# One-core causal attention and squared-ReLU MLP: v's loads as four operations of their own, and a last output block turned on TensorE

## The chip, the cores and the metric

The kernel runs on one core of one Trainium2 chip. The metric is the device time of one execution in microseconds (us); "the time" of a kernel is the median over its runs.

## The reference, cut to what matters

```python
# q, k, v: (4, 12, 448, 64); w_in: (768, 2048); w_out: (2048, 768), all float32
scores = (q @ k.transpose(0, 1, 3, 2)) / 8
scores = np.where(np.triu(ones, k=1), -1e9, scores)
attn = exp(scores - max(scores)); attn = attn / (sum(attn) + 1e-9)
o = attn @ v
x = o.transpose(0, 2, 1, 3).reshape(1792, 768)
h = np.maximum(x @ w_in, 0.0)
out = (h * h) @ w_out                      # (1792, 768)
```

## The kernel before, in words

**The work.** Attention goes by pairs of heads: pair n (0 to 23) is batch n // 6 and heads 2 (n % 6) and the next. For each pair the kernel loads q and k by eight DMAs in 32-column strips (`load_qk`, L343, four for k and four for q, 56 KB each), turns them in 32 x 32 blocks on VectorE (`transposed`, L366), makes scores on TensorE (`scores`, L381 to L388), takes the maximum on VectorE (L399), the exponential on ScalarE (L403), divides on GpSimd or VectorE (L412, L414), turns the probabilities on TensorE (`transposed_p`, L426), copies them out of PSUM (L433, which calls L311, or L434) and multiplies by v (`times_v`, L446). Pairs 0 to 11 (two batches) come first, with two sets of buffers; pairs 12 to 23 run between the matmuls of the MLP.

v is loaded for three pairs at a time (NV = 3) into one of two buffers, by `load_v` (L355), in pairs 0, 3, 6, 9, ...: four DMAs, one for each block of 128 keys (kc), 192 KB for a full one and 96 KB for the last, in rows of 256 bytes, all issued by one operation on SP's queue.

The MLP keeps every float32 operand as two parts (high and low) in float32r, and a product is three matmuls. The first half of the rows goes straight through it in four groups of 512 of the 2048 hidden columns (`h_unit`, L628; `o_unit`, L1000). The weights come in pieces (`piece`, L560): w_in has six pieces c = 0 to 5 a group. A piece's words are loaded (L587; 512 KB for w_in, 384 KB for w_out), ScalarE makes two parts of them (L590, L593, both by way of L311), VectorE puts them together (L595 to L598), and `split` (L327) makes high and low. The second half of the rows goes by a scheme with seven products for eight (`h_pair`, L803; `o_seven`, L949). For the last group `o_last` (L978) makes the eight products as they are: twelve blocks, three (d) for each of four quarters (k) of the sums; a block is twelve matmuls (L941 to L943). Its sum is added on VectorE (L986, which calls L314) to the tile of sums, turned on VectorE in 32 x 32 blocks (L988), and stored by four DMAs in rows of 128 bytes (L993), two on SP's queue and two on ScalarE's. The last block is (k, d) = ("22", 2).

**What sets the order.** Each step is an operation of a planner (`Plan.op`, L72) with a rank (a due time in us), the engines that it may run on with a modelled length, and keys that it reads and writes. `Plan.emit` (L100) walks through time: among the operations that are ready it takes the one that can start first, and among equals the one of lowest rank; a DMA is held back while more than a set backlog (L46) is under way. `take=` reserves a buffer and `drop=` gives it back. The instructions are then put out in that order, and each engine and each queue works through its own in order. Nearly all loads are on SP's queue ("DMA"), a few at the start and some stores at the end on ScalarE's ("DMA2").

Pair n has the time n x 8.6 for n below 12 (PAIR, L1037). Its k and q have that time less 14 as rank (L349). Its v has the time less 4 for n = 0 and less 10 after that (L364). The load of w_in's piece c in group 0 has 10 + 97.2 x (c + 0.5) / 6 - 12 (L1056, L587), but there are only three buffers for the words. `times_v` reads the whole v buffer as one key.

The buffers of the last stages are made late: `grow` (L1102), an operation on POOL of no modelled length, opens a pool in place of an older one.

Of the kernel before, what the change touches and what calls it, by code (L numbers as in the profile page):

```python
# [9 lines left out]
F32 = mybir.dt.float32  # L10
# [5 lines left out]
ALU = mybir.AluOpType  # L16

PE, ACT, DVE, POOL, DMA, DMA2 = range(6)
# [6 lines left out]
class Hold:  # L25
# [5 lines left out]
    @property  # L31
    def t(self):
        t = self.tile[1]
        return t() if isinstance(t, FunctionType) else t
# [127 lines left out]
def t_act(n, psum=False, more=0):  # L162
    return n / 1200 + (0.17 if psum else 0.215) + 0.15 * more


def t_dve(n, fast=False):
    return n / 1920 + 0.15 if fast else n / 960 + 0.15
# [13 lines left out]
def t_dma(count, size):  # L181
    return count * (0.0084 + size * 0.0000488) / 16
# [3 lines left out]
def kernel(  # L186
# [17 lines left out]
    nc = tc.nc  # L204
    B, H, S, D = q.shape
    DM = out.shape[1]
    DFF = w_in.shape[1]
    P = 128
    QC = P // 2
    NQ = S // QC  # L210
    NK = -(-S // P)
    NP = H // 2
    NPH = B // 2
    T = 2 * S
# [3 lines left out]
    CH = DM // 2  # L218
# [14 lines left out]
    TURNED = [(c, kc) for kc in range(NK) for c in range(2 * kc, NQ)]  # L233
    TOFF = [P * next(i for i, t in enumerate(TURNED) if t[1] == kc) for kc in range(NK)]
    NV = 3
    NA = 2 * NP
    PCW = max(GF * P, CH)
    NRAW, NZ, NB, NR = 3, 3, 1, 6
# [2 lines left out]
    CB = NP // 2  # L241
# [18 lines left out]
    plan = Plan()  # L260

    def tiles(nm, n, shape, dtype, pool=const):
        return [pool.tile(shape, dtype, name=f"{nm}{i}") for i in range(n)]

    early = ExitStack()
    pool = early.enter_context(tc.tile_pool(name="early", bufs=1, side="right"))
    ident = pool.tile([P, 3 * QC], F32, name="ident")
    mask = pool.tile([P, S], F32, name="mask")
    even = Buffers("a", pool)
    v_t = tiles("v", 2, [P, NK, 2 * NV, D], F32, pool)  # L270
    x_t = tiles("x", NA, [P, 2, S], F32R)
    wi_t = const.tile([P, 2, NP, GF * P], F32R, name="wi")
# [28 lines left out]
    for i in range(2):  # L301
        m = mask[i * QC:(i + 1) * QC, S - QC:]
        nc.gpsimd.affine_select(
            out=m, in_=m, pattern=[[-1, QC]], base=0,
# [5 lines left out]
    def on_act(n, dst, src, psum=False, func=AF.Copy, more=0, **kw):  # L310
        return (ACT, t_act(n, psum, more), lambda: nc.scalar.activation(dst(), src(), func, **kw))  # L311

    def on_dve(n, dst, a, b, op, more=0.0):
        return (DVE, t_dve(n) + more, lambda: nc.vector.tensor_tensor(out=dst(), in0=a(), in1=b(), op=op))  # L314
# [22 lines left out]
    def attention(s, n, at):  # L337

        b, hp = divmod(n, NP)
        nm = s.nm  # L340
        spare = (lambda us: us) if n >= NA else (lambda us: 0.0)

        def load_qk(key, src, t, j):  # L343


            queue, eng = (DMA2, nc.scalar) if n < 2 and key == "q" else (DMA, nc.sync)
            for h in range(D // SQ):
                i = (j * D + h * SQ)
                plan.op(at - 14, [(queue, 0.5, lambda h=h, i=i: eng.dma_start(  # L349
                    out=t[i:i + SQ].rearrange("p (b d) -> p b d", d=SQ),  # L350
                    in_=src[b, 2 * hp + j, :, h * SQ:(h + 1) * SQ].rearrange(
                        "(b p) d -> p b d", p=SQ),
                ), t_dma(S, 128))], [], [(nm, key, j, h)])

        def load_v():  # L355
            hold = vs[n // NV] = Hold("v", "v")

            def go():
                for kc in range(NK):
                    rows = min(P, S - kc * P)  # L360
                    nc.sync.dma_start(
                        out=hold.t[:rows, kc],
                        in_=v[b, 2 * hp:2 * (hp + NV), kc * P:kc * P + rows].rearrange("h p d -> p h d"))
            plan.op(at - (10 if n > 1 else 4), [(DMA, 0.5 * NK, go, t_dma(2 * NV * S, 256))], [], [hold], take=hold)  # L364

        def transposed(key, src, dst, at):  # L366
            plan.op(at, [(DVE, t_dve(S), lambda: nc.vector.transpose(dst, src))],
# [69 lines left out]
        def times_v(av, at):  # L437

            first = 2 * (n % NV)

            def go():
                for kc in range(NK):
                    m = NQ - 2 * kc
                    p = s.pt[:, TOFF[kc]:TOFF[kc] + m * P].rearrange("p (c j i) -> p c j i", j=2, i=QC)
                    for j in range(2):
                        nc.tensor.matmul(  # L446
                            av.t[j * D:(j + 1) * D, kc * P:S], vr.t[:, kc, first + j], p[:, :, j],
                            start=kc == 0, stop=kc == NK - 1, skip_group_check=True,
                        )
            plan.op(at, [(PE, 0.2 + 4 * sum((S - kc * P) / 2400 for kc in range(NK)), go)],  # L450
                    [vr] + [(nm, "pt", i) for i in range(len(TURNED) // 4)], [av], take=av, drop=[vr],
                    lag=spare(1.0))

        for j in range(2):
# [1 line left out]
        for j in range(2):  # L456
            load_qk("q", q, s.q, j)
        if n % NV == 0:
            load_v()
        vr = vs[n // NV]  # L460
        transposed("k", s.k, s.kt, at)
        transposed("q", s.q, s.qt, at + 1)
        at += 4
        groups = (ORDER[:3], ORDER[3:]) if n < NA else (ORDER,)
        for chunks in groups:
# [11 lines left out]
        av = Hold("ps", "av")  # L477
# [3 lines left out]
        at += 3  # L481
        if n < NA:
            x = x_t[n]
# [5 lines left out]
        else:  # L489
            spill(n - NA, av, at)  # L490

# [51 lines left out]
    late = {"wo": None, "acc": None}  # L543
# [389 lines left out]
    def o_sum(k, d):  # L933
        return lambda: late["sum"][("u2", "11", "12", "21", "22").index(k) * CB + d]

    def o_product(ps, pairs, d, begin, end, rank, step):

        for m, (w, g) in enumerate(pairs):
            def go(w=w, g=g, start=begin and m == 0, stop=end and m == len(pairs) - 1):
                o = ps.t[:, :S]  # L940
                nc.tensor.matmul(o, w.t[:, 0, d], g.t[:, 0], start=start, stop=False, skip_group_check=True)  # L941
                nc.tensor.matmul(o, w.t[:, 0, d], g.t[:, 1], start=False, stop=False, skip_group_check=True)  # L942
                nc.tensor.matmul(o, w.t[:, 1, d], g.t[:, 0], start=False, stop=stop, skip_group_check=True)  # L943
            plan.op(rank, [(PE, 3 * t_mm(S), go)], [(w, 0), (w, 1), (g, 0), (g, 1)], [ps],
                    take=ps if begin and m == 0 else None, drop=[w, g])
            rank += step
        return rank
# [30 lines left out]
    def o_last(W, rank, step):  # L978

        for k in ("11", "21", "12", "22"):  # L980
            i, j = k
            for d in range(CB):
                ps, a = Hold("ps", "os"), o_sum(k, d)
                rank = o_product(ps, [(W[i + m, u], g7[TURNS[-1], m + j, u]) for m in "12" for u in range(2)],
                                 d, True, True, rank, step)
                plan.op(rank, [on_dve(S, a, lambda ps=ps: ps.t[:, :S], a, ALU.add)], [ps], [("sum", k, d)], drop=[ps])  # L986
                h = Hold("f", "tr")
                plan.op(rank, [(DVE, t_dve(S) + 0.05, lambda h=h, a=a: nc.vector.transpose(h.t, a()))],  # L988
                        [("sum", k, d)], [h], take=h)
                row, col = T + (int(j) - 1) * S, (int(i) - 1) * CH + d * P  # L990
                for s in range(P // SQ):
                    def go(eng, h=h, s=s, row=row, col=col):
                        return lambda: eng.dma_start(  # L993
                            out=out[row:row + S, col + s * SQ:col + (s + 1) * SQ].rearrange(
                                "(b p) d -> p b d", p=SQ),
                            in_=h.t[s * SQ:(s + 1) * SQ].rearrange("p (b d) -> p b d", d=SQ))
                    plan.op(rank, [(DMA, 0.6, go(nc.sync), t_dma(S, 128)), (DMA2, 0.6, go(nc.scalar), t_dma(S, 128))], [h], [], drop=[h])
        return rank

    def o_unit(gr, t, ch, rank, step, after):  # L1000
        ps = Hold("ps", "mm")
# [38 lines left out]
    odd = Buffers("b", stack.enter_context(tc.tile_pool(name="b", bufs=1)))  # L1040
    for n in range(NA):
        attention((even, odd)[n % 2], n, n * PAIR)
# [37 lines left out]
    rank, begin = start, 10.0  # L1080
    rest = NG * (2 * GF * NP * H_US + 2 * NT * GF * O_US) - GF * NP * H_US
    for gr in range(NG):
        begin, rank = group(gr, rank, (rest + NA * 7.0) / rest, begin)
# [18 lines left out]
    def grow():  # L1102
        middle.close()
        pool = ctx.enter_context(tc.tile_pool(name="third", bufs=1, reuse_waits="tile"))
        late["g"] = tiles("g3_", 4, [P, 2, S], F32R, pool)
        late["w"] = pool.tile([P, 2, CB, P], F32R, name="w3")
        late["f"] = tiles("f3_", 4, [P, S], F32, pool)
        late["sum"] += tiles("sb", 4 * CB, [P, S], F32, pool)

    grown = over(plan.ops[:mark] + [attended], lent_w[2 * GF:] + lent_f[-1:] + lent_r + lent_g, grow)  # L1110
# [10 lines left out]
    for gr, u in stages:  # L1121
        last = gr == TURNS[-1]
        if u is None:
            W = o_parts(gr, rank - LEAD, rank + 42 * H_US - LEAD)
            rank = o_last(W, rank, H_US) if last else o_seven(gr, W, rank, H_US)
        else:
            W = w_parts(gr, u, rank - LEAD, rank + 7 * CB * H_US - LEAD)
            rank = h_pair(gr, u, W, rank, H_US, last)
# [33 lines left out]
```

## Time and profile before

| | us |
|---|---|
| median of three runs | 615.32 |
| the runs | 617.53, 615.32, 612.15 |
| the profiled execution | 616.32 |
| its span, first to last instruction | 614.5 |
| TensorE matmul busy in it | 589.6 (96%) |
| VectorE, ScalarE, GpSimd busy | 442.8, 357.3, 353.8 |
| mean granted TensorE clock | 0.994 |

The profile is one execution, taken by the hardware profiler. All times in it count from the first instruction. An engine's idle time ahead of an instruction is given in brackets with what ended it. Engines: PE is TensorE, DVE is VectorE, ACT is ScalarE, POOL is GpSimd, SP is SyncE; "SPq" and "ACTq" are instructions of a queue that issue DMAs; L12 is line 12 of the kernel. The granted clock is a share of TensorE's full 2.4 GHz; the lower level, 1.2 GHz, reads 0.5. Matmuls overlap each other, so a matmul's own time is longer than its distance from the next.

### The profile page before, as it was taken

The numbers are of one execution on the slowest core, as the hardware profiler recorded it, in microseconds if no ns is written. First come the engines' busy times: TensorE is split into PE (matmuls) and PEld (weight loads), VectorE is DVE, ScalarE is ACT, GpSimd is POOL, SyncE is SP. The second block draws the span as 40 slices with busy tenths as digits, with TensorE's granted clock in tenths as the row PEclk, the third lists the DMA queues.
The fourth block names the chain that finished last, engine by engine and source line by source line (L and its number), as shares of the span: only waits on it lengthen the run. The fifth ranks groups of instructions, "written<-read, shape, count | busy, mean of one in ns | idle before, by whom it ended". The sixth has DMA issues, their size and how long they took to land.

```text
span 614.5 us, 11394 instructions
## 1 busy us (share of the span) xinstructions
PE 589.6 (96%) x3714; PEld 511.1 (83%) x3714; DVE 442.8 (72%) x958; ACT 357.3 (58%) x878; POOL 353.8 (58%) x459
## 2 busy tenths in 40 slices
PE   3897999999999999999999999999999999999996
PEld 1564677789988988888898889988889999999995
DVE  4888785466786689785787327678996688779754
ACT  3797888656677855578455552255675743652400
POOL 2557575475579746788644764325894666575200
PEclk9899999999999999999999999999999999999999
DMA  8897745597989999989997477867877847863555
GB/s 141 174 208 134 170 105 117 107 306 259 245 230 263 283 267 213 272 254 298 242 282 249 158 204 221 283 196 208 190 139 173 207 120 145 184 151 66 166 91 90
DMA packets 203148, 120.01 MB, mean 195 GB/s; under 512 B 138960, under 2 KB 191056, under 8 KB 203088
## 3 DMA queue, kind: packets, MB, share of 16 engines
q1 hardware_dynamic: 181328, 108.01, 64.2%
q0 software_dynamic: 6912, 9.44, 10.3%
q10 hardware_dynamic: 14848, 1.84, 1.9%
q8 instruction: 29, 0.48, 0.3%
q14 instruction: 31, 0.25, 0.1%
HBM read 80.71 MB, written 38.54 MB: 194 GB/s over the span
## 4 chain that ended last, share of the span: by engine, by line
PE 83%; DVE 7%; DMA 4%; ACT 2%; issue 2%; POOL 1%; SPq 1%; DVEq 0%; ACTq 0%; POOLq 0%
PE ps L1014 7%; PE ps L634 7%; PE ps L1016 6%; PE ps L1015 6%; PE ps L636 6%; PE ps L635 6%; PE ps L426 6%; PE ps L446 6%; PE ps L386 5%; PE ps L941 5%; PE ps L942 5%; PE ps L943 5%; PE ps L819 4%; PE ps L817 4%; PE ps L815 4%
## 5 line engine op out<-in xcount | busy, mean ns | idle before, releaser
L412 POOL TENSOR_SCALAR ap<-ap,asm 128x128 f32<-128x128 f32 (+6 forms) x122 | 72.8, 616 | 53.3 <-DVE asm L471 51.5
L311 ACT ACTIVATE words<-words 128x384 f32<-128x384 f32 (+3 forms) x131 | 75.1, 598 | 28.1 <-DVE words L314 8.3
L399 DVE CUSTOM_DVE_ANT_0 ps<-ps,mask 128x448 f32<-128x448 f32 (+6 forms) x168 | 68.7, 445 | 30.4 <-PE ps L386 23.9
L1014 PE MATMUL ps<-wo,g 128*128 128x384 f32 x224 | 77.0, 344 | 0.0
L634 PE MATMUL ps<-x,wi 128*128 128x448 f32 x192 | 75.0, 391 | 0.6 <-ACT x L311 0.6
L1016 PE MATMUL ps<-wo,g 128*128 128x384 f32 x224 | 75.1, 335 | 0.0
L1015 PE MATMUL ps<-wo,g 128*128 128x384 f32 x224 | 75.0, 335 | 0.0
L636 PE MATMUL ps<-x,wi 128*128 128x448 f32 x192 | 70.8, 369 | 0.4 <-DVE wi L314 0.4
L635 PE MATMUL ps<-x,wi 128*128 128x448 f32 x192 | 70.6, 368 | 0.2 <-DVE x L314 0.2
L318 POOL TENSOR_TENSOR wi<-words,wi 128x384 fp32r<-128x384 f32 (+1 forms) x48 | 62.6, 1326 | 8.8 <-ACT wi L311 6.0
L403 ACT ACTIVATE ap<-ps,mx 128x448 f32<-128x448 f32 (+6 forms) x126 | 58.7, 483 | 13.6 <-DVE mx L399 12.6
L324 POOL TENSOR_SCALAR wi<-words 128x384 fp32r<-128x384 f32 (+1 forms) x44 | 32.0, 730 | 51.6 <-DVE words L598 14.4
L815 PE MATMUL ps<-x,wi 128*128 128x448 f32 x153 | 56.4, 368 | 0.8 <-DVE r L314 0.5
L817 PE MATMUL ps<-x,wi 128*128 128x448 f32 x153 | 56.1, 367 | 0.0
L819 PE MATMUL ps<-x,wi 128*128 128x448 f32 x153 | 56.1, 366 | 0.0
L941 PE MATMUL ps<-g,wi 128*128 128x448 f32 x150 | 55.0, 367 | 0.5 <-ACT sa L311 0.5
L943 PE MATMUL ps<-g,wi 128*128 128x448 f32 x150 | 54.9, 366 | 0.0
L942 PE MATMUL ps<-g,wi 128*128 128x448 f32 x150 | 54.8, 366 | 0.0
L311 ACT ACTIVATE r<-ps 128x448 f32<-128x448 f32 x59 | 32.1, 546 | 38.3 <-PE ps L636 13.6
L314 DVE CUSTOM_DVE_ANT_0 words<-words 128x768 uint16<-128x768 uint16 (+1 forms) x56 | 45.8, 818 | 5.3 <-ACT words L311 1.9
L311 ACT ACTIVATE apt<-ps 128x512 f32<-128x512 f32 x70 | 38.5, 605 | 18.2 <-PE ps L426 18.1
L311 ACT ACTIVATE r<-r 128x448 f32<-128x448 f32 x64 | 36.0, 575 | 14.8 <-DVE r L314 14.0
(140 smaller groups left out, 1475.0 us busy)
## 6 DMA issues: line engine op xcount, KB each, us to landing
words<-in_moe_w_in_dram SPq DMA_DIRECT2D x24, 512.0 KB, 5.5
words<-in_moe_w_out_dram SPq DMA_DIRECT2D x32, 384.0 KB, 4.5
wo_split<-wo SPq DMA_DIRECT2D x26, 384.0 KB, 4.5
wi<-wo_split SPq DMA_DIRECT2D x21, 384.0 KB, 4.0
wo_whole<-words SPq DMA_DIRECT2D x32, 192.0 KB, 3.9
wi_split<-wi SPq DMA_DIRECT2D x24, 256.0 KB, 4.1
v<-in_v_dram SPq DMA_DIRECT2D x24, 192.0 KB, 4.0
wi_whole<-words SPq DMA_DIRECT2D x18, 256.0 KB, 4.6
```

Source lines behind the costliest of these rows:

```text
L311: return (ACT, t_act(n, psum, more), lambda: nc.scalar.activation(dst(), src(), func, **kw))
L634: nc.tensor.matmul(o, w[:, 0], x[:, 0], start=c == 0, stop=False)
L635: nc.tensor.matmul(o, w[:, 0], x[:, 1], start=False, stop=False)
L636: nc.tensor.matmul(o, w[:, 1], x[:, 0], start=False, stop=c == NP - 1)
L815: nc.tensor.matmul(o, w.t[:, 0, c], x[:, 0], start=begin and c == 0, stop=False, skip_group_check=True)
L817: nc.tensor.matmul(o, w.t[:, 0, c], x[:, 1], start=False, stop=False, skip_group_check=True)
L941: nc.tensor.matmul(o, w.t[:, 0, d], g.t[:, 0], start=start, stop=False, skip_group_check=True)
L942: nc.tensor.matmul(o, w.t[:, 0, d], g.t[:, 1], start=False, stop=False, skip_group_check=True)
L943: nc.tensor.matmul(o, w.t[:, 1, d], g.t[:, 0], start=False, stop=stop, skip_group_check=True)
L1014: nc.tensor.matmul(res(), g[:, 0], w[:, 0], start=f == 0, stop=False)
L1015: nc.tensor.matmul(res(), g[:, 0], w[:, 1], start=False, stop=False)
L1016: nc.tensor.matmul(res(), g[:, 1], w[:, 0], start=False, stop=f == GF - 1)
```

## The change

v's loads: `load_v` now makes one operation that only takes the buffer (on POOL, of no length and without an instruction) and four that issue one DMA each. V_AT gives the rank of the first by the pair (0 to -4, as before; from pair 3 on -4 and not -10), and each further one is 2 us later. `times_v` reads the four as four keys.

The last block: `finish` takes the place of the add, the 32 x 32 turn and the four stores. It works in two parts, columns 0 to 255 and 256 to 447 of the block. Each is added on VectorE, turned by two TensorE transposes into a PSUM bank, and copied out: the first part by one copy on ScalarE, the second by two on VectorE. The first part is stored by one DMA on ScalarE's queue (256 rows), the second by two on SP's queue (128 and 64 rows), in rows of 512 bytes. The transposes need an identity, which is made by GpSimd in `grow`.

```diff
+    V_AT, V_STEP = (-4, -10, -4), 2
...
         def load_v():
             hold = vs[n // NV] = Hold("v", "v")
 
-            def go():
-                for kc in range(NK):
-                    rows = min(P, S - kc * P)
+            taken = plan.op(at + V_AT[min(n, 2)], [(POOL, 0.0, lambda: None)], [], [(hold, kc) for kc in range(NK)], take=hold)
+            for kc in range(NK):
+                def go(kc=kc, rows=min(P, S - kc * P)):
                     nc.sync.dma_start(
                         out=hold.t[:rows, kc],
                         in_=v[b, 2 * hp:2 * (hp + NV), kc * P:kc * P + rows].rearrange("h p d -> p h d"))
-            plan.op(at - (10 if n > 1 else 4), [(DMA, 0.5 * NK, go, t_dma(2 * NV * S, 256))], [], [hold], take=hold)
+                plan.op(at + V_AT[min(n, 2)] + V_STEP * kc, [(DMA, 0.5, go, t_dma(2 * NV * min(P, S - kc * P), 256))],
+                        [], [(hold, kc)], [taken])
...
-                    [vr] + [(nm, "pt", i) for i in range(len(TURNED) // 4)], [av], take=av, drop=[vr],
+                    [(vr, kc) for kc in range(NK)] + [(nm, "pt", i) for i in range(len(TURNED) // 4)], [av], take=av, drop=[vr],
...
+                if (k, d) == ("22", CB - 1):
+                    finish(ps, a, d, rank)
+                    continue
...
+    def finish(ps, a, d, rank):
+        row, col = T + S, CH + d * P
+        for first, end in ((0, 2 * P), (2 * P, S)):
+            turned, h = Hold("ps", "os"), Hold("f", "tr")
+            def part(t, first=first, end=end):
+                return lambda: t()[:, first:end]
+            plan.op(rank, [on_dve(end - first, part(a), part(lambda: ps.t), part(a), ALU.add)],
+                    [ps, ("sum", "22", d)], [("sum", "22", d, first)], drop=[ps])
+            def turn(first=first, end=end, turned=turned):
+                for m in range(first, end, P):
+                    n = min(P, end - m)
+                    nc.tensor.transpose(turned.t[:n, m - first:m - first + P], a()[:, m:m + n], late["ident"])
+            plan.op(rank, [(PE, 0.22, turn)], [("sum", "22", d, first)], [turned], take=turned)
+            blocks = [(0, 2, P)] if first == 0 else [(0, 1, P), (1, 1, S - 3 * P)]
+            for m, count, n in blocks:
+                def dst(m=m, count=count, n=n, h=h):
+                    return h.t[:n, m * P:(m + count) * P]
+                def src(m=m, count=count, n=n, turned=turned):
+                    return turned.t[:n, m * P:(m + count) * P]
+                copy = [(DVE, t_dve(P), lambda dst=dst, src=src: nc.vector.tensor_copy(dst(), src()))]
+                plan.op(rank, copy if first else [on_act(2 * P, dst, src, True)],
+                        [turned], [(h, m)], plan.ops[-2:-1] if m else (), take=None if m else h, drop=[turned])
+                def store(eng, m=m, count=count, n=n, dst=dst, first=first):
+                    r = row + first + m * P
+                    return lambda: eng.dma_start(
+                        out=out[r:r + count * n, col:col + P].rearrange("(b p) d -> p b d", p=n),
+                        in_=dst().rearrange("p (b d) -> p b d", d=P))
+                plan.op(rank, [(DMA, 0.4, store(nc.sync), t_dma(n * count, 512)) if first else
+                               (DMA2, 0.4, store(nc.scalar), t_dma(n * count, 512))], [(h, m)], [], drop=[h])
...
+        late["ident"] = pool.tile([P, P], F32, name="ident3")
+        make_identity(nc, late["ident"])
         late["sum"] += tiles("sb", 4 * CB, [P, S], F32, pool)
```

## Rows read from the trace of the kernel before

**Rows 1.** Windows: length; busy us and instructions of each engine; granted clock; DMA.
```profile
40.00:60.00 20.00, 16.19 (x153) 11.23 (x146) 17.43 (x55) 15.76 (x47) 15.26 (x27) 1.00 0.82 173
60.00:80.00 20.00, 19.58 (x149) 14.14 (x150) 15.47 (x48) 17.89 (x55) 12.06 (x20) 0.91 0.81 170
...
125.00:250.00 125.00, 125.00 (x851) 110.78 (x848) 94.45 (x212) 83.06 (x207) 82.52 (x100) 1.00 0.92 260
```

**Rows 2.** Timeline of TensorE: start, length, instruction, [idle before it <- what ended it].
```profile
46.34 1.95 PE L446 MATMUL ps<-bpt,v 128*64 128x448 f32 x16
...
59.95 1.83 PE L426 MATMUL ps<-ident,bp 128*128 128x128 f32 x8 [2.99 <-ACT ap L403]
...
73.84 1.95 PE L446 MATMUL ps<-apt,v 128*64 128x448 f32 x16
```

**Rows 3.** Timeline of ScalarE around 58 us.
```profile
57.97 1.23 ACT L311 ACTIVATE words<-words 128x512 f32<-128x512 f32 x2 [3.52 <-DMA words<-in_moe_w_in_dram]
```

**Rows 4.** Timeline of SP's queue: start, length, DMAs issued, how many.
```profile
18.79 2.46 SPq L361 DMA_DIRECT2D v<-in_v_dram  x4
...
29.90 0.48 SPq L587 DMA_DIRECT2D words<-in_moe_w_in_dram  x1
30.47 2.30 SPq L349 DMA_DIRECT2D bq<-in_q_dram  x4
32.88 2.55 SPq L349 DMA_DIRECT2D ak<-in_k_dram  x4
...
37.62 0.90 SPq L587 DMA_DIRECT2D words<-in_moe_w_in_dram  x2
39.09 5.09 SPq L361 DMA_DIRECT2D v<-in_v_dram  x4
44.23 1.65 SPq L349 DMA_DIRECT2D bk<-in_k_dram  x3
...
48.07 1.99 SPq L349 DMA_DIRECT2D ak<-in_k_dram  x4
...
52.24 0.42 SPq L587 DMA_DIRECT2D words<-in_moe_w_in_dram  x1
52.76 2.80 SPq L349 DMA_DIRECT2D bk<-in_k_dram  x4
55.65 3.16 SPq L349 DMA_DIRECT2D bq<-in_q_dram  x4
```

**Rows 5.** Timeline of TensorE and VectorE at the end.
```profile
608.84 0.37 PE L943 MATMUL ps<-g,wi 128*128 128x448 f32 x1
609.24 0.62 DVE L314 TENSOR_TENSOR sb<-ps,sb 128x448 f32<-128x448 f32 x1 [1.13 <-PE ps L943]
609.90 0.65 DVE L988 STREAM_TRANSPOSE words<-sb 128x448 f32<-128x448 f32 x1
```

**Rows 6.** The output's stores from 609.9 us on: issue lengths, first and last start.
```profile
L993 SPq DMA_DIRECT2D out_dram<-words x2: 316/398/481, 610.6 to 610.9; - x2
L993 ACTq DMA_DIRECT2D out_dram<-words x2: 375/434/493, 610.6 to 611.0; - x2
...
DMA to landing us min/median/max: 1.8/2.1/2.4
```

**Rows 7.** Durations: eight and four transposes (timeline); copies by form (busy, mean ns).
```profile
78.57 0.60 PE L426 MATMUL ps<-ident,bp 128*128 128x128 f32 x4
...
80.23 1.04 PE L426 MATMUL ps<-ident,bp 128*128 128x128 f32 x8
...
L311 ACT ACTIVATE sb<-ps 128x448 f32<-128x448 f32 x12 | 6.0, 546 | 1.8 <-PE ps L943 1.8
...
L1026 DVE COPY acc<-ps 128x384 f32<-128x384 f32 x4 | 2.2, 554 | 2.1 <-PE ps L1016 2.1
L434 DVE COPY apt<-ps 128x512 f32<-128x512 f32 x2 | 1.3, 672 | 4.3 <-PE ps L426 4.3
```

**Rows 8.** Timeline of POOL around 404 us.
```profile
403.83 0.57 POOL L324 TENSOR_SCALAR g<-r 128x448 fp32r<-128x448 f32 x1 [13.97 <-ACT r L311]
```

## Prediction

> **What bounds the kernel now.** I read the busy time of each engine by stage first. From 40 to 60 us TensorE works 16.19 of 20 us, from 60 to 80 it works 19.58, and from 125 to 250 us all of 125.00 [rows 1]. After the first 80 us there is nothing to win by feeding TensorE earlier; what can move is the idle time ahead of that, and what lies behind the last matmul. So next come the waits in TensorE's timeline: one stands out, 2.99 us ahead of the transposes that begin at 59.95, ended by ScalarE [rows 2]. In ScalarE's timeline the cause stands one step back: at 57.97 it takes up the last of the six w_in pieces (c = 5) of group 0, after 3.52 us in which it waited for that piece's load [rows 3]. The third view is SP's queue: that load leaves it only at 52.24, at the end of a queue that has had no pause. Four k or q loads take it 1.99 us when nothing holds them (48.07), and the four v loads of pair 3 take 2.46 (18.79), but those of pair 6 take 5.09 (39.09), right behind two w_in loads of 512 KB at 37.62 [rows 4]. Behind the hole the clock falls: it is 0.91 over 60 to 80 us [rows 1], that is, part of that stretch ran at the lower of the two levels, which costs about 20 x 0.09 = 1.8 us. The last matmul begins at 608.84 and ends at 609.21 [rows 5], and the span ends at 614.5: a tail of 5.3 us.
>
> **Part 1: v's loads.** For pair 0 the ranks go from -4 to -4, -2, 0, 2. The next load in line, k of pair 2, has 2 x 8.6 - 14 = 3.2, so nothing changes place. For pair 3 (time 25.8) they go from 15.8 to 21.8, 23.8, 25.8, 27.8, and pair 4's k and q (20.4) and the w_in piece c = 1 (22.3) come between: these can start up to 2.5 us earlier, the time that v's four take SP there [rows 4]. TensorE reads this v at 46.34 [rows 2], some 20 us behind its new place, so nothing becomes late, and I cost this at 0 because no idle of TensorE in the rows ends on those loads. For pair 6 (51.6) they go from 41.6 to 47.6 ... 53.6, behind pair 7's k and q (46.2) and still ahead of pair 8's (54.8). In the trace three of pair 7's four k loads follow v, at 44.23 [rows 4], and its four q loads come after them; all seven will now pass v. This v is first read at 73.84 [rows 2], so it too has time. The number of loads ahead of c = 5 stays the same: seven k and q loads and four v loads change places, and no instruction is added to SP's queue (v was four DMAs before). The new operation named on POOL issues nothing. From pair 9 on the moves lie beside a TensorE that is busy 19.58 of 20 and 125.00 of 125 us; I cost them at 0.
>
> What can change is how long the queue stands. V's four loads behind the two 512 KB loads take 5.09 - 2.46 = 2.6 us more than the same four did at 18.79. If that is a price of big transfers standing together, it goes, and c = 5 leaves up to 2.6 us earlier. If it is a price of whatever stands behind the w_in loads, the k and q loads take it over. Rows for that: behind the single w_in load at 29.90 the next eight take 2.30 + 2.55 against twice 1.99, 0.9 more; behind the one at 52.24 they take 2.80 + 3.16, 2.0 more [rows 4]. Two loads together might cost their followers 1.2 to 2.0, which leaves a gain of 0.6 to 1.4. I take 1.0; the ends are 2.6 of gain, and, when the price doubles with the two loads, 2 x 2.0 - 2.6 = 1.4 of loss. ScalarE's wait of 3.52 falls with it one for one and so does TensorE's 2.99, since ScalarE's work ahead of it doesn't move. The lower clock stays: the hole is still 2 us. Early part: -1.0 us.
>
> Every order of the planner may shift with these loads. Apart from the hole, the two windows hold 3.81 - 2.99 + 0.42 = 1.2 us of idle TensorE [rows 1]: that is my bound, either way, for what a new order of the other work can bring or cost.
>
> **Part 2: the last block.** Before: add 609.24 to 609.86, transpose 609.90 to 610.55 [rows 5], two stores on each of two queues from 610.6, the last issued at 611.0, and the slowest of them lands after 2.4 us [rows 6], at 613.4; the remaining 1.1 us to the end of the span is closing work that stays. After: an add of 256 columns, an add of 192, each followed by a pair of TensorE transposes, a copy out of PSUM (ScalarE for the first half, two copies on VectorE for the second), and stores. Lengths: the copies of 512 and 384 columns differ by 672 - 554 = 118 ns [rows 7], 0.92 ns a column, so the adds take 0.62 - 192 x 0.00092 = 0.44 and 0.38, and a copy of 128 columns 0.32. ScalarE copies 448 columns in 0.546 [rows 7]; with the same slope 256 take 0.37. Eight transposes take 1.04 and four 0.60 [rows 7], 0.11 each and 0.16 on top: a pair takes 0.38. A hand-over costs about 0.04 (609.86 to 609.90).
>
> First half: add to 609.68, transposes 609.73 to 610.11, ScalarE's copy 610.15 to 610.52, store issued at 610.55. Second half: add 609.70 to 610.08, transposes 610.13 to 610.51, copies 610.55 to 610.87 and to 611.19, stores issued at 610.9 and 611.25. The last store leaves 0.25 us later than now. It moves 64 rows of 512 bytes where each of the four moved 448 x 4 pieces of 128. The shortest landing of the window is 1.8 us, with 56 KB each [rows 6]; with 32 KB, and only three stores about, I take that: 611.25 + 1.8 = 613.05 against 613.4, so -0.35, say -0.4. Bounds: at the 2.4 us of now it is +0.25; if both copies run beside the store of the first half and land like it, -0.9. The identity for these transposes is two short POOL instructions where POOL stands idle for 13.97 us ahead of 403.83 [rows 8]; without that cover they would cost well under 1 us on an engine that is not the bound.
>
> The row says that transposes in a row stand 0.11 us apart. The Trainium skill (TensorE: Matmul & The Clock Gate, "Part 4: PE-mode transpose") speaks against the detour: the result lands in PSUM, so a copy must follow, and it gives some 275 ns for one in a kernel. By that figure a pair would be about 0.55 us, an estimate, and the tail 0.17 longer than mine. No number above uses it.
>
> **Sum.** The profiled execution took 616.32 us, 1.0 above the median of the runs, 615.32. -1.0 - 0.4 makes 614.9 of it, and 613.9 of the median, which is my prediction.
>
> **Rivals.**
> 1. The whole price goes: c = 5 leaves 2.6 us earlier, TensorE's hole shrinks to 0.4, and the lower clock behind it goes too. -2.6 - 1.8 - 0.4: 610.5. For it: v's loads are twice as big as k's and stand right behind the two big ones. Against: k and q loads are slowed behind a w_in load too [rows 4].
> 2. Nothing is won early, and a store lands in its fixed time however its rows are cut: +0.25, 615.6. For it: the landings of the window lie close together (1.8 to 2.4). The Trainium skill (DMA: Bandwidth & Descriptors, "Latency and other measured facts") holds that the confirmation from HBM is most of a DMA's cost of about 2 us; no row parts it from the moving of the data.
> 3. Slower: the k and q loads, now directly behind the two w_in loads, are held 2 x 2.0 us, and v then stands right ahead of pair 8's loads and c = 5, which leaves 1.4 us later. ScalarE's wait grows to 4.9, TensorE's hole to 4.4: 615.3 + 1.4 - 0.4 = 616.3. It decides from the point where the eight lose more than 2.6 us. For it: 2.0 behind one load at 52.24. Against: 0.9 at 29.90.
> 4. The move is none: the planner takes the operation that can start first and looks at ranks only among equals, so v's parts may fill places where k or q is not yet free, as they did. Then only the tail counts: 614.9. Against: pair 7's k loads were under way when v came between them, so they were free.
>
> **How the numbers follow.** The forecast has 0.5, rival 1 0.17, rival 2 0.15, rival 3 0.13, rival 4 0.05. With the 1.2 us of new order on either side rival 1 reaches 609.3 and rival 3 617.5; the range is 610.0 to 617.4. A measurement of this kernel tells about 1%, 6.2 us, from no change: faster means under 609.2, slower over 621.5. Faster needs rival 1 with luck in the order, 0.09; slower needs rival 3 at several times its price, 0.05; the rest, 0.86, is within 1%.
>
> **What would show it.** Right: in SP's timeline pair 7's eight loads stand together ahead of pair 6's v; c = 5 is issued near 51 and not 52.2; ScalarE's wait for it is about 2.5 us and TensorE's hole about 2. The last store is issued near 611.25 on the clock of the trace above (2.0 us behind the last matmul) and the span ends 4.9 us behind the last matmul instead of 5.3. Wrong: a hole of under 1 us and no lower clock at 60 us (rival 1), a hole of over 3 us (rival 3), a tail over 5.3 us (rival 2), or TensorE idle later than 80 us.

## The result and the profile after

| | before | after |
|---|---|---|
| median, runs side by side (17 each) | 617.53 us | 611.87 us |
| ratio, 95% interval | | 0.992 (0.9903 to 0.9938) |
| the profiled execution | 616.32 us | 611.87 us |
| its span | 614.5 us | 610.1 us |
| end of the last product to the end of the span | 5.29 us | 5.05 us |
| mean granted TensorE clock in it | 0.994 | 0.996 |

One of the 17 executions of the change took 832.43 us at a mean granted clock of 0.661 and is left out of the ratio, which is that of the means of the rest (611.9 against 616.8 us). The change takes 0.8% off, some 4.9 us of 617.5. The forecast was 1.4 us less, the range 610.0 to 617.4 around 613.9: the direction and the range held, the size did not. Most of the difference stands ahead of 80 us. Windows of the kernel after (length; busy us and instructions of PE, PEld, DVE, ACT, POOL; granted clock; DMA share, GB/s), to be read beside [rows 1]:

```profile
20.00:40.00 20.00, 18.45 (x172) 11.40 (x165) 16.68 (x58) 17.84 (x57) 11.12 (x21) 1.00 0.81 157
40.00:60.00 20.00, 18.06 (x146) 12.14 (x145) 16.66 (x56) 16.06 (x48) 11.48 (x21) 0.91 0.87 172
60.00:80.00 20.00, 19.39 (x175) 12.82 (x176) 18.57 (x58) 18.13 (x56) 12.37 (x21) 1.00 0.95 186
```

And the window of the kernel before that [rows 1] did not have:

```profile
20.00:40.00 20.00, 17.92 (x158) 11.87 (x154) 16.98 (x57) 16.75 (x52) 9.33 (x17) 0.91 0.86 169
```

From 40 to 60 us TensorE is busy 18.06 us where it was 16.19. The low clock stood in two of these windows before (0.91 and 0.91, about 1.8 us each) and stands in one after. The busy time cannot be taken for time won one for one: from 0 to 20 us the two profiles count 80 and 79 matmuls and read 8.79 and 9.84 us busy, both at a clock of 1.00. The hole itself is seen in the queue and the timelines. SP's queue after, to be read beside [rows 4]:

```profile
39.11 0.90 SPq L589 DMA_DIRECT2D words<-in_moe_w_in_dram  x2
40.13 2.28 SPq L350 DMA_DIRECT2D bk<-in_k_dram  x4
42.51 3.51 SPq L350 DMA_DIRECT2D bq<-in_q_dram  x4
46.13 0.41 SPq L589 DMA_DIRECT2D words<-in_moe_w_in_dram  x1
46.64 4.22 SPq L362 DMA_DIRECT2D v<-in_v_dram  x4
50.95 2.34 SPq L350 DMA_DIRECT2D ak<-in_k_dram  x4
53.38 3.59 SPq L350 DMA_DIRECT2D aq<-in_q_dram  x4
```

Pair 7's eight loads now stand together, as forecast. But behind them comes the load of c = 5, at 46.13 and not at 52.24, and only then pair 6's v and pair 8's eight. It has passed twelve loads. ScalarE's timeline after, to be read beside [rows 3]: the first of these rows is its work on c = 3, with a wait, the second that on c = 5, without one.

```profile
43.76 0.67 ACT L312 ACTIVATE words<-words 128x512 f32<-128x512 f32 x1 [2.74 <-DMA words<-in_moe_w_in_dram]
...
54.18 0.69 ACT L312 ACTIVATE words<-words 128x512 f32<-128x512 f32 x1
```

TensorE's timeline after, to be read beside [rows 2]:

```profile
44.96 4.01 PE L388 MATMUL ps<-bkt,bqt 64*64 64x448 f32 x28 [1.83 <-ACT bpt L312]
...
56.31 1.95 PE L448 MATMUL ps<-apt,v 128*64 128x448 f32 x16
58.19 0.66 PE L428 MATMUL ps<-ident,bp 128*128 128x128 f32 x4
58.61 0.45 PE L636 MATMUL ps<-x,wi 128*128 128x448 f32 x1
```

The hole of 2.99 us ahead of 59.95 is gone. A smaller one, 1.83 us, has come ahead of 44.96, behind ScalarE's wait of 2.74 for c = 3, which leaves SP 1.5 us later than before (39.11 against 37.62). The low clock now stands in the window of this smaller hole, 40 to 60 us.

The end after, to be read beside [rows 5, 6]: TensorE, VectorE and ScalarE from their timelines, then the stores.

```profile
604.68 0.37 PE L945 MATMUL ps<-g,wi 128*128 128x448 f32 x1
605.56 0.70 PE L1020 MATMUL ps<-ident,sb 128*128 128x128 f32 x4 [0.52 <-DVE sb L315]
```
```profile
605.08 0.69 DVE L315 TENSOR_TENSOR sb<-ps,sb 128x256 f32<-128x256 f32 x2 [1.13 <-PE ps L945]
606.30 0.48 DVE L1029 COPY words<-ps 128x128 f32<-128x128 f32 x2 [0.53 <-PE ps L1020]
```
```profile
606.04 0.38 ACT L312 ACTIVATE words<-ps 128x256 f32<-128x256 f32 x1 [27.68 <-DMA out_dram<-words]
606.45 0.43 ACTq L1035 DMA_DIRECT2D out_dram<-words  x1
```
```profile
L1035 SPq DMA_DIRECT2D out_dram<-words x2: 350/442/534, 606.6 to 607.1; - x2
L1035 ACTq DMA_DIRECT2D out_dram<-words x1: 434/434/434, 606.5 to 606.5; - x1
...
DMA to landing us min/median/max: 1.9/2.1/2.1
```

The last product ends at 605.05, the last store is issued at 607.1, 2.0 us behind it (1.8 before), and the three stores land after 1.9 to 2.1 us although they move 32 to 128 KB in wide rows.

### The profile page after: what moved, and what is told of

Same layout as the page of the kernel before. It is cut to its first block, busy times and chain, and to the rows that moved or that the text cites. A ratio compares the mean times of both kernels' runs of the same rounds, so it can differ in the third digit from the quotient of the medians.

```text
span 610.1 us, 11412 instructions
## 1 busy us (share of the span) xinstructions
PE 591.2 (97%) x3718; PEld 510.7 (84%) x3718; DVE 447.0 (73%) x961; ACT 357.6 (59%) x880; POOL 350.7 (57%) x459
## 4 chain that ended last, share of the span: by engine, by line
PE 84%; DMA 5%; DVE 4%; ACT 3%; issue 1%; SPq 1%; POOL 1%; DVEq 0%; ACTq 0%
PE ps L636 7%; PE ps L1055 7%; PE ps L1057 6%; PE ps L1056 6%; PE ps L448 6%; PE ps L638 6%; PE ps L637 6%; PE ps L388 6%; PE ps L428 6%; PE ps L943 5%; PE ps L945 5%; PE ps L944 5%; PE ps L821 4%; PE ps L819 4%; PE ps L817 4%; DMA words<-in_moe_w_in_dram 1%
## 5 line engine op out<-in xcount | busy, mean ns | idle before, releaser
L319 POOL TENSOR_TENSOR wi<-words,wi 128x384 fp32r<-128x384 f32 (+1 forms) x47 | 60.3, 1308 | 8.5 <-ACT wi L312 6.9
L597 DVE TENSOR_SCALAR words<-words 128x384 int32<-128x384 int32 (+1 forms) x56 | 31.9, 573 | 25.3 <-ACT words L312 19.2
L315 DVE CUSTOM_DVE_ANT_0 words<-words 128x768 uint16<-128x768 uint16 (+1 forms) x56 | 44.2, 789 | 6.7 <-ACT words L312 3.2
```

## The experiments

Theory A: the gain is the place of one load. c = 5, which ScalarE waits for in order, leaves SP ahead of pair 8's k and q loads. Theory B: it is v's later place as such. Theory C: it is the new order that the planner gives to the work on the other engines. Ratios are to runs of the kernel before on the same chip (their medians were 616.42, 616.28 and 616.25 us in the three sets), with 95% intervals.

**The first part alone (v_only).**

```diff
-                if (k, d) == ("22", CB - 1):
-                    finish(ps, a, d, rank)
-                    continue
...
-        late["ident"] = pool.tile([P, P], F32, name="ident3")
-        make_identity(nc, late["ident"])
```

> The change without its second part: v's loads as in the change, the last block as before. If the parts add up and the tail gives what the two profiles show (0.3 us), this takes some 4.5 us off the kernel before, a ratio of 0.9925 to 0.994. If the second part were worth more than its tail, the ratio is above 0.996.

Measured: 613.05 us, 0.9942 (0.9922 to 0.9962), a little less than expected. The first part carries the gain, as far as the intervals tell.

**The second part alone (finish_only).** `load_v` and the keys of `times_v` as before, `finish` as in the change.

```diff
-            taken = plan.op(at + V_AT[min(n, 2)], [(POOL, 0.0, lambda: None)], [], [(hold, kc) for kc in range(NK)], take=hold)
...
+            plan.op(at - (10 if n > 1 else 4), [(DMA, 0.5 * NK, go, t_dma(2 * NV * S, 256))], [], [hold], take=hold)
```

> The change without its first part: v's loads as before, the last block as in the change. From the profiles: the time behind the last product falls by 0.3 us and nothing else moves, a ratio of 0.9995; 0.4 was predicted, with +0.25 and -0.9 as ends. A ratio under 0.997 would say that the second part does more than that.

Measured: 615.69 us, 1.0001 (0.9977 to 1.0024). No gain can be seen. Its end in the trace, SP's queue and the landings:

```profile
607.08 1.28 SPq L1034 DMA_DIRECT2D out_dram<-words  x2
```
```profile
L1034 SPq DMA_DIRECT2D out_dram<-words x2: 351/445/539, 607.1 to 607.8; - x2
L1034 ACTq DMA_DIRECT2D out_dram<-words x1: 417/417/417, 606.9 to 606.9; - x1
...
DMA to landing us min/median/max: 1.9/2.1/2.1
```
```profile
605.14 0.37 PE L944 MATMUL ps<-g,wi 128*128 128x448 f32 x1
```

The last product ends at 605.51 and the span at 610.9, 5.4 us behind it: here the two stores on SP take 1.28 us and not 0.98, the last one goes out 2.3 us behind the product, and the landing is the same. With the four DMAs of before the tail is 5.2 to 5.4 us in the profiles; with `finish` it is 5.0 to 5.5 in five.

This profile also shows how far the hole changes from one execution to another. SP's queue is that of the kernel before, and c = 5 leaves it at 52.69, even 0.45 us later. But the load lands 4.3 us after its issue, where it took 5.6 in the profile before. ScalarE takes it up at 57.08 (its row names POOL as what ended the wait, but the load had landed only at 57.0), and TensorE's hole is 2.08 us:

```profile
57.08 1.23 ACT L312 ACTIVATE words<-words 128x512 f32<-128x512 f32 x2 [2.62 <-POOL bp L413]
```
```profile
59.06 1.42 PE L427 MATMUL ps<-ident,bp 128*128 128x128 f32 x8 [2.08 <-ACT ap L404]
```

The clock from 60 to 80 us is 1.00 behind it, and the execution took 612.64 us, the least of the twelve. So a profile shows what waits for what; what a change is worth is told by the runs.

**One load moved (c5_early).** This and the later moves leave the planner's result as it is and take single operations to another place in the list that is put out:

```diff
         order.sort(key=lambda x: x[:2])
+        for moved, anchor in self.moves:
+            first = [x for x in order if x[2] in moved]
+            rest = [x for x in order if x[2] not in moved]
+            at = [x[2] for x in rest].index(anchor) + 1
+            order = rest[:at] + first + rest[at:]
...
+    plan.moves.append(([named["i", 0, 5]], named["q", 7]))
```

> The kernel before with one thing changed: the load of the w_in piece c = 5 leaves SP ahead of pair 8's eight k and q loads, right behind pair 7's; v and the order of every other instruction stay. Theory A (what counts is that this load passes those eight): it leaves near 48 us and not at 52.2, ScalarE's wait of 3.5 us and TensorE's hole of 3.0 near 57 us go or fall under 1 us, and with the hole a stretch at the lower clock: 2.5 to 4.5 us less, a ratio of 0.993 to 0.996. Theory B (what counts is v's later place): nothing changes, as v stays. Theory C (the planner's new order of the other work): nothing changes either.

Measured: 613.22 us, 0.9945 (0.9925 to 0.9964). SP's queue and TensorE's timeline:

```profile
46.65 2.46 SPq L354 DMA_DIRECT2D bq<-in_q_dram  x4
49.22 0.41 SPq L593 DMA_DIRECT2D words<-in_moe_w_in_dram  x1
49.73 1.94 SPq L354 DMA_DIRECT2D ak<-in_k_dram  x4
```
```profile
51.89 0.66 PE L431 MATMUL ps<-ident,ap 128*128 128x128 f32 x4 [0.73 <-DVE x L319]
58.22 0.88 PE L431 MATMUL ps<-ident,bp 128*128 128x128 f32 x6 [0.29 <-POOL bp L417]
```

c = 5 leaves 3.0 us earlier, and the hole of 2.99 is down to 0.29, with a new one of 0.73 ahead of 51.89. One load in another place, with v where it was and nothing else moved, gives as much as the whole first part: theory A holds, and neither B nor C is needed.

**v moved, pair 8's loads still ahead (v6_behind_c5).**

```diff
+    plan.moves.append(([named["v", 6]], named["i", 0, 5]))
```

> The kernel before with one thing changed: the four v loads of pair 6 go out behind the w_in piece c = 5 and not ahead of it; pair 8's k and q loads still stand ahead of c = 5, and the order of every other instruction stays. Theory A: c = 5 leaves SP earlier only by what v's four took there, 2.5 to 5 us, and the hole near 57 us shrinks by as much: 2 to 4 us less. Theory B: the same size, since v is out of the way. If big loads only hand their delay on to the loads behind them (the taken-over price of the prediction), c = 5 leaves 1 us earlier or less: 0 to 1 us less. Theory C: nothing.

Measured: 612.07 us, 0.992 (0.9888 to 0.9951), 4.9 us less where 2 to 4 were expected. c = 5 leaves at 50.51:

```profile
46.34 2.00 SPq L354 DMA_DIRECT2D ak<-in_k_dram  x4
48.43 1.99 SPq L354 DMA_DIRECT2D aq<-in_q_dram  x4
50.51 0.42 SPq L593 DMA_DIRECT2D words<-in_moe_w_in_dram  x1
51.03 4.40 SPq L366 DMA_DIRECT2D v<-in_v_dram  x4
```
```profile
55.30 1.32 ACT L316 ACTIVATE words<-words 128x512 f32<-128x512 f32 x2 [0.16 <-POOL bp L418]
```
```profile
58.24 0.88 PE L432 MATMUL ps<-ident,bp 128*128 128x128 f32 x6 [0.29 <-POOL bp L418]
```

Only 1.7 us earlier on SP, yet the hole is gone here too. The trace adds it up. The load lands 4.7 us after its issue and not 5.6, so at 55.2 us and not at 57.9, and ScalarE, whose earlier work ends 0.7 us later here, is free for it at 55.14 and not at 54.45: its wait falls from 3.52 to 0.16 (the row names POOL as what ended it, but POOL's work on bp runs on to 58.2, and the landing at 55.2 fits). That the landing is shorter because v's loads stand behind this load is not shown, for in finish_only, with v's loads ahead of it, it took 4.3. v counts by what it puts in front of c = 5. The price is partly handed on, as the prediction's rows said: counted from the issue of c = 3, which left 0.9 us later here than before (38.48 against 37.62), c = 5 leaves 2.6 us earlier, of the 5.1 that v's loads took. What the prediction held fixed is the time from issue to landing.

**The change with this load put back (after_c5_back).**

```diff
+    plan.moves.append(([named["i", 0, 5]], named["q", 8]))
```

> The changed kernel with one thing put back: the load of the w_in piece c = 5 goes out behind pair 8's eight k and q loads, as it did before the change; all else as in the changed kernel. Theory A (the gain is this load's place): it leaves SP 4 to 6 us later than 46.1, ScalarE waits for it again and TensorE gets a hole of 2 to 4 us near 55 us; 3 to 5 us are lost again, a ratio to the kernel before of 0.997 to 1.002. Theory B (v's later place) and theory C (new order of the other work): the ratio stays at 0.992 to 0.994.

Measured: 618.42 us, 1.0033 (1.0012 to 1.0054). SP's queue, ScalarE's and TensorE's timelines:

```profile
53.08 0.42 SPq L595 DMA_DIRECT2D words<-in_moe_w_in_dram  x1
```
```profile
57.45 0.66 ACT L317 ACTIVATE words<-words 128x512 f32<-128x512 f32 x1 [3.75 <-DMA words<-in_moe_w_in_dram]
```
```profile
58.64 1.76 PE L393 MATMUL ps<-akt,aqt 64*64 64x256 f32 x12 [3.58 <-ACT apt L317]
```

With this one load back behind pair 8's the hole is there again, 3.58 us, and the whole gain is lost with it, a little more even: theories B and C are out as causes of the gain.

**Split, with the old ranks (split_same_rank).**

```diff
-    V_AT, V_STEP = (-4, -10, -4), 2
+    V_AT, V_STEP = (-4, -10, -10), 0
```

and the last block as before.

> Only the splitting: v's loads are four operations behind one that takes the buffer, but with the ranks of the kernel before (10 us ahead for pairs 3 and on, step 0); the last block as before. Theory A with its cause in the splitting: an operation behind another becomes ready 1.7 us after it in the planner, and c = 5, which is ready, slips in ahead of v and so ahead of pair 8's loads; c = 5 leaves SP near 46 to 48 us, no hole over 1 us near 57 us, 3 to 4.5 us less, a ratio of 0.993 to 0.995. If the later ranks make the gain, the ratio is 0.998 to 1.002.

Measured: 611.72 us, 0.9924 (0.9899 to 0.9949). SP's queue:

```profile
42.07 3.94 SPq L350 DMA_DIRECT2D bq<-in_q_dram  x4
46.12 0.41 SPq L589 DMA_DIRECT2D words<-in_moe_w_in_dram  x1
46.63 4.88 SPq L362 DMA_DIRECT2D v<-in_v_dram  x4
```

The later ranks are not needed: the splitting does it. How it does so is read from the planner's code and was not run by itself. Before, v's one operation took the buffer itself and could start as soon as this was free. Now an operation on POOL takes it, which in the planner must also wait until POOL is free, and the loads are ready only 0.3 us (LAG) and 1.4 us (ISSUE) after it. In this gap c = 5, which waits for no other operation, can start first, as pair 8's loads are not ready yet either. What a splitting without the operation on POOL would do was not measured.

**Later, in one piece (one_late).**

```diff
-            plan.op(at - (10 if n > 1 else 4), [(DMA, 0.5 * NK, go, t_dma(2 * NV * S, 256))], [], [hold], take=hold)
+            plan.op(at - 4, [(DMA, 0.5 * NK, go, t_dma(2 * NV * S, 256))], [], [hold], take=hold)
```

> Only the later rank: v's four DMAs stay one operation, at 4 us ahead and not 10; the last block as before. In the planner's order v then stands behind pair 7's loads, and c = 5 right behind v and ahead of pair 8's. Theory A: c = 5 leaves SP at 49 to 50.5 us, ahead of 52.2; ScalarE's wait of 3.5 falls to 1 or less, 2.5 to 4.5 us less, a ratio of 0.993 to 0.996. If only the splitting can bring it, the ratio is 0.998 or more.

Measured: 613.52 us, 0.9964 (0.9939 to 0.999), just outside what was expected.

```profile
47.60 0.55 SPq L587 DMA_DIRECT2D words<-in_moe_w_in_dram  x1
```
```profile
54.57 0.97 PE L386 MATMUL ps<-akt,aqt 64*64 64x256 f32 x12 [1.21 <-ACT apt L311]
```

c = 5 leaves at 47.60, behind v and ahead of pair 8's loads. So the rank alone also brings the load forward past pair 8's eight, though not past v's four, with a gain that reads smaller (the two intervals overlap); the profile keeps a hole of 1.21 us near 54 us.

**Nearly the queue of the change, and nothing else of it (queue_after).**

```diff
+    plan.moves.append(([named["v", 3]], named["i", 0, 1]))
+    plan.moves.append(([named["i", 0, 5]], named["q", 7]))
+    plan.moves.append(([named["v", 6]], named["i", 0, 5]))
```

> The kernel before with SP's queue of the changed kernel and nothing else of it: pair 3's v goes out behind c = 1, c = 5 behind pair 7's loads, pair 6's v behind c = 5; the order on every other engine and the last block stay as before. Theory A: the whole of the first part's gain or more, 3.5 to 5 us, a ratio of 0.992 to 0.9945. Theory C (it takes the new order on the engines too): a ratio over 0.997.

Measured: 612.03 us, 0.9928 (0.9901 to 0.9955).

```profile
47.73 0.41 SPq L594 DMA_DIRECT2D words<-in_moe_w_in_dram  x1
48.24 4.16 SPq L366 DMA_DIRECT2D v<-in_v_dram  x4
```
```profile
46.23 3.80 PE L392 MATMUL ps<-bkt,bqt 64*64 64x448 f32 x28 [2.00 <-ACT bpt L316]
```

The queue is not quite that of the change: there the first of pair 3's four v loads stays ahead of pair 4's, at 18.65, and only three go behind c = 1, where here all four do; and beyond 60 us the queue is the one of before. With that said, the order of the loads ahead of 60 us gives the whole gain, with the order on every other engine left alone.

**Pair 3's v alone (v3_behind_c1).**

```diff
+    plan.moves.append(([named["v", 3]], named["i", 0, 1]))
```

> The kernel before with one thing changed: pair 3's four v loads go out behind the w_in piece c = 1 and not ahead of pair 4's k and q loads. c = 5 keeps its place. The hole of 3.0 us near 57 us stays. In the four kernels where pair 3's v stood behind c = 1, ScalarE waited 1.9 to 2.9 us for c = 3 and TensorE had a hole of 1.2 to 2.0 near 44 us, which the kernels with this v in its old place had not or at 0.7. Theory D (this part of the move costs): such a hole appears, 0 to 2 us more, a ratio of 1.000 to 1.003. If the hole near 44 comes from pair 6's v, none appears and the ratio is 0.999 to 1.001.

Measured: 616.76 us, 1.0006 (0.9975 to 1.0036). ScalarE's timeline and TensorE's:

```profile
45.80 0.67 ACT L316 ACTIVATE words<-words 128x512 f32<-128x512 f32 x1 [3.40 <-DMA words<-in_moe_w_in_dram]
```
```profile
47.00 3.57 PE L392 MATMUL ps<-bkt,bqt 64*64 64x448 f32 x28 [1.40 <-ACT bpt L316]
62.79 1.45 PE L432 MATMUL ps<-ident,bp 128*128 128x128 f32 x6 [2.53 <-ACT ap L409]
```

The first of TensorE's rows is a new hole, 1.40 us near 46 us, behind ScalarE's wait of 3.40 for c = 3, which leaves at 40.58 and not at 37.62; the second is the old one, 2.53 us, ended by ScalarE. So this part of the move can bring such a hole, as theory D has it. It is not the only thing that does, though: split_same_rank, with pair 3's v in its old place, has one of 1.16 us too, with c = 3 leaving at 38.79 (the low ends of the expectation, 1.9 and 1.2 us, are of this kernel).

```profile
44.56 2.80 PE L388 MATMUL ps<-bkt,bqt 64*64 64x448 f32 x28 [1.16 <-ACT bpt L312]
```

A price of this part can't be told from nothing, and neither can a gain.

**Two versions meant to beat both (place_c5_v6, place_c3_c5_v6).** The kernel before with `finish` and these moves; the second has the first line too.

```diff
+    plan.moves.append(([named["i", 0, 3]], named["q", 5]))
+    plan.moves.append(([named["i", 0, 5]], named["q", 7]))
+    plan.moves.append(([named["v", 6]], named["i", 0, 5]))
```

> Meant to beat both: the kernel before with the last block of the change, c = 5 sent out behind pair 7's loads and pair 6's v behind c = 5, and pair 3's v left in its old place. By theory A the hole near 57 us goes; by theory D the one near 44 us is 0.7 or less: 4 to 6 us less than before, a ratio of 0.990 to 0.9935. If pair 3's move had a gain of its own, this is slower than the changed kernel, over 0.9935.

Measured: 611.44 us, 0.9924 (0.9899 to 0.9949). c = 5 leaves at 44.57, and the hole near 44 us is 0.36.

> The same, and c = 3 sent out ahead of pair 6's k and q loads (right behind pair 5's q), as its buffer has been free since 23 us. Theory A carried on (a w_in piece late on the queue holds ScalarE, a k or q load does not): ScalarE waits under 0.5 us for any w_in piece, the hole near 44 us goes, 4.5 to 7 us less than before, a ratio of 0.989 to 0.993. If the small holes are not on the path, the same as the run beside it.

Measured: 611.65 us, 0.9928 (0.9903 to 0.9953). ScalarE waits for no w_in piece from 30 us on. Neither is told apart from the change. With c = 5 in time, the smaller hole near 44 us can't be seen in the time: the ratio is 0.9924 with 1.16 us of it (split_same_rank), 0.9924 with 0.36 and 0.9928 without.

## Why the prediction was right in direction and too small

**What bounds the kernel.** This reading held: one hole, ended by ScalarE's wait for c = 5, which stood too late on SP's queue. after_c5_back shows it best: this load's place is the whole gain. The size of the hole was read from one execution: 2.99 us there, 2.08 in finish_only with the same queue.

**The early term, -1.0.** This is the one that was mis-sized. The first part took off about 3.6 us (0.9942 of 616.4; 2.3 to 4.8 by the interval), and 4.4 in queue_after, which has nearly its order of loads ahead of 60 us. The step that failed is "The number of loads ahead of c = 5 stays the same". I ordered the loads by rank, and by rank c = 5 (87.1) comes behind v and behind pair 8's loads. But the planner looks first at what can start, and only then at ranks. I used that rule in rival 4 and not here. Either half of the change lets c = 5 pass pair 8's eight (one_late, split_same_rank); the splitting lets it pass v's four as well. "The new operation named on POOL issues nothing" was true, and by the planner's code it is what opened the gap: it costs no instruction, but it changes what is ready.

**Big loads behind big loads.** The rows for a handed-on price were right in kind: pair 7's loads behind c = 3 and c = 4 take 2.28 + 3.51, 1.8 us more than twice 1.99, within the 1.2 to 2.0 forecast. Yet this hardly mattered, since c = 5 passed twelve loads.

**The lower clock.** I left it where it was. It stood in two windows before and in one after, so one stretch of 1.8 us went. With the hole at 44 us a new stretch came. Here the sum was short a second time: the mean granted clock of the runs was 0.993 before and 0.996 in v_only and in c5_early beside it (medians on one chip), some 1.8 us by 0.003 of 616, an estimate.

**Pair 3's move, 0.** No idle of TensorE ended on these loads, but in the changed kernel c = 3 leaves 1.5 us later, and there ScalarE waits 2.74 us and TensorE 1.83. The runs tell no price of it from zero.

**The tail, -0.4.** The lengths were good: the last store was issued 2.0 us behind the last product, as forecast, and the two halves of the sum, transposes and copies took 0.2 us less or more at most. The estimate of 0.55 us for a pair of transposes, worked out from a bfloat16 figure of the Trainium skill (TensorE: Matmul & The Clock Gate, "Part 4: PE-mode transpose"), was too long here: four float32 ones, the last of 64 columns, took 0.70 us together. The landing of 1.8 us was too hopeful: 1.9 to 2.1 us for 32 to 128 KB in wide rows, where 56 KB in narrow ones took 1.8 to 2.4 (each of the four stores of before was 448 pieces of 128 bytes, and not 448 x 4). The profile of the change gains 0.2, that of finish_only nothing, and the runs tell none of it from zero. Rival 2 described this part better. The rule of the Trainium skill beside it (DMA: Bandwidth & Descriptors, "Latency and other measured facts"), that the confirmation and not the data makes most of a small store's time, fits these landings, which lie within 0.2 us of each other for 32 to 128 KB; no row parts the confirmation from the data.

**Rivals.** Rival 1 gave 610.5, and the ratio times the median of the first runs, 0.992 x 615.32, is 610.4: its two effects came (no hole at 57 us, one low stretch fewer), but not by its mechanism, for v's price behind the big loads didn't vanish: v's four still took 4.22. Rival 3 failed: c = 5 left earlier. Rival 4's premise was right and its conclusion wrong: the planner's first rule made the move work.

## What to carry to other kernels

In a list scheduler an operation split in two changes when its second half is ready, and whatever is ready in that gap goes first, whatever its rank: follow the whole queue, not only the operation that was moved. When an engine that works in order waits for a load, count the loads ahead of that one load; place a load by who waits for it and how long its consumer can do without. A shorter chain at the end must beat the nearly fixed time of a store, and 0.2 us of it can't be seen in a time of 612.

## What the runs showed of the hardware that I had not expected

The granted clock is not a fixed property of the kernel. The kernel before read 0.989 to 0.997 in the 29 runs beside the last set (median 0.994), the change 0.992 to 1.0 in its 16 runs of some 612 us (median 0.9975), but in another set. Side by side on one chip, in the first set, the kernel before read 0.987 to 0.999 in 27 runs (median 0.993) and c5_early, with one load moved, 0.995 to 0.997 in 11 (median 0.996). The difference of 0.003 is some 1.8 us of 616, an estimate, where c5_early gains 3.4: by it, about half of that gain comes through fewer stretches at 1.2 GHz, ahead of which TensorE had stood idle in the profiles. Which idle time brings one varies: with the same waits of 3.2 us near 10 us, the window from 20 to 40 us read 0.91 in the profile before and 1.00 in the profile after, and behind holes of 2.99 and 2.08 us near 57 us the window from 60 to 80 us read 0.91 (before) and 1.00 (finish_only).
